# Whole-array transposes and output products, and later stores, in an attention and token-mixing kernel

## The chip, the core and the metric

The kernel runs on one core of a Trainium2 chip. The core has a matrix engine (TensorE; PE for its matmuls, PEld for its weight loads), VectorE (DVE), ScalarE (ACT), GpSimd (POOL) and SyncE (SP), each with its own instruction stream in order, and 16 DMA engines. The metric is device time in microseconds (us).

## The reference

It is a block-wise linear attention with decay, followed by a token-mixing layer. There are 4 batches, 8 heads, 768 positions and 64 columns a head. In the attention, with `Dmask[i, j] = lam ** (i - j)` for `i >= j`:

```python
intra = einsum('bhij,bhjd->bhid', einsum('bhic,bhjc->bhij', qb, kb) * Dmask, vb)
inter = einsum('bhid,bhde->bhie', qb * lam_pow, kv_state)
out[:, :, sl] = intra + inter
kv_state = lam_block * kv_state + einsum('bhsd,bhse->bhde', kb_dec, vb)
```

The heads are then laid side by side, so that `x` is 4 x 768 x 512, and

```python
W_tok = einsum('bsd,btd->bst', x @ w_q, x @ w_k) / 8
out = maximum(einsum('bst,btd->bsd', W_tok, x), 0) @ w_out
```

Inputs and output are float32; the kernel computes in bfloat16 with float32 sums.

## The kernel before

**Pairs.** The work is cut into 16 pairs of heads, n = 0 to 15; batch b = n // 4, pair of the batch kk = n % 4. Positions are cut into six chunks of 128, the decay is folded into q (`Dq`) and v (`DvI`), and one loop over n writes the order of every engine's work out by hand (the pools run under a manual schedule, so program order is engine order).

**What a pair does.** `turn` (L208) transposes q and k of a pair on PE; VectorE writes qT with the decay (L225), ScalarE copies kT (L242). `scores` (L285) makes four PSUM tiles sc, `masks` (L298) multiplies them by the causal mask on VectorE, two tiles each call. `states` (L255) makes the running key-value sums dps; VectorE brings them to gs in three steps (L265 to L267). `inter` (L308) and `values` (L329) add up the attention output in oa, and ScalarE copies it, transposed, to xT (L341). `flip` (L350) transposes xT back to xnat, position-major, copied by ScalarE in batch 0 and for the last pair (L355), else by VectorE (L357).

**Mixing.** Once a batch is whole, `mix_wk` (L371) and `mix_wq` (L390) make the two projections, `mix_py` (L410) the product of wk and x, whose copy is Y (L419, L425). `mix_pm` (L442) makes the mixed rows, ScalarE or VectorE puts them through the relu to rmT (L462, L453). `mix_po` (L473) is the product with w_out, one tile of 128 positions at a time: in `mix_po` and in `flip` each matmul uses 64 columns of weights and writes half of the PSUM partitions, so two are issued for each 128. The tile goes to osb (L484, L482) and is stored by SP at once (L485).

**The order.** The mixing of batch p = b - 1 is spread over the pairs of batch b, by the table at L532: `rows` and `quarters` are calls of `mix_pm`, `one` and `two` are lists of other products that stand in the middle and at the end of a pair's work. For n < 8 a pair's order on PE is rows, scores, wk, states, flip(n-1), one, turn(n+1), inter, quarters, values, two. For n >= 8 it is rows, scores, wk, inter, quarters, flip(n-1), turns, one, values, states(n+1), two (at n = 7 states(8) is made as well). What is left of batches 2 and 3 follows the loop (L587 on).

**Loads.** POOL issues the loads of q, k and v, which turn float32 into bfloat16 on the way (L74, L79), six pairs ahead, and scales v in between (`scale_v`, L193). SP issues the first loads, the weights w_q and w_k, and the stores.

**PSUM.** All tiles but oa come from one pool of six slots (`pst`); a tile waits until the one that held its slot has been read. The output tiles osb have four slots.

Of the kernel before, what the change touches and what calls it, by code (L numbers as in the profile page):

```python
# [27 lines left out]
def kernel(  # L28
# [18 lines left out]
    gsp = ctx.enter_context(tc.tile_pool(name="gsp", bufs=3))  # L47
    xtp = ctx.enter_context(tc.tile_pool(name="xtp", bufs=2))
    hyp = ctx.enter_context(tc.tile_pool(name="hyp", bufs=2))
    outp = ctx.enter_context(tc.tile_pool(name="outp", bufs=4))  # L50
    ps = ctx.enter_context(tc.tile_pool(name="ps", bufs=6, space=bass.MemoryType.PSUM))
    psx = ctx.enter_context(tc.tile_pool(name="psx", bufs=2, space=bass.MemoryType.PSUM))
    ctx.enter_context(tc.manual_schedule())
# [136 lines left out]
    def scale_v(n, eng):  # L190
        b, kk = pairs[n]
        vn = nat.tile([128, 2, NCH, D], BF16, tag="vn", name="vn")
        eng.tensor_tensor(  # L193
            out=vn,
            in0=staged.pop((n, "v")),
            in1=DvI[:, 2 * kk : 2 * kk + 2, :].unsqueeze(3).to_broadcast([128, 2, NCH, D]),
            op=ALU.mult,
        )
        L[n]["vn"] = vn
# [95 lines left out]
    def masks(n, a):  # L295
        for hl in range(2):
            t = prb.tile([128, 3, CH], BF16, tag="pr", name="pr")
            nc.vector.tensor_tensor(out=t, in0=L[n]["sc"][a, hl], in1=maskc, op=ALU.mult)  # L298
            L[n]["pr"][a, hl] = t
# [44 lines left out]
    def flip(n):  # L344
        b, kk = pairs[n]
        xp = pst([128, NCH, CH], BF16, "xp")
        for t in range(NCH):
            for i in range(2):
                o = t * CH + i * 64
                nc.tensor.transpose(  # L350
                    xp[i * 64 : i * 64 + 64, t, :], xT[b][:, kk, o : o + 64], ident
                )
        to = xnat[b][:, :, kk * CH : (kk + 1) * CH]
        if b == 0 or n == N - 1:
            nc.scalar.copy(out=to, in_=xp)  # L355
        else:
            nc.vector.tensor_copy(out=to, in_=xp)  # L357
# [7 lines left out]
    def mix_wk(b, kts=range(NP)):  # L365
        if 0 in kts:
            M[b] = dict(wk=pst([128, NCH, DHY], F32, "wk"))
        wk = M[b]["wk"]
        for t in range(NCH):
            for kt in kts:  # L370
                nc.tensor.matmul(  # L371
                    wk[:, t, :],
                    xT[b][:, kt, t * CH : (t + 1) * CH],
                    wqk[:, 1, kt, :],
                    start=(kt == 0 and (t == 0 or len(kts) == NP)),
                    stop=(kt == NP - 1),
                    skip_group_check=True,
                )
        if NP - 1 in kts:
            wkn = hyp.tile([128, NCH, DHY], BF16, tag="wkn", name="wkn")  # L380
            nc.vector.tensor_copy(out=wkn, in_=wk)
            M[b]["wkn"] = wkn

    def mix_wq(b, kts=range(NP)):
        if 0 in kts:
            M[b]["wq"] = pst([128, HALF], F32, "wq")
        wq = M[b]["wq"]
        for kt in kts:
            for n in range(2):
                nc.tensor.matmul(  # L390
                    wq[n * 64 : n * 64 + 64, :],
                    wqk[:, 0, kt, :],
                    xT[b][:, kt, n * HALF : (n + 1) * HALF],
                    start=(kt == 0),
                    stop=(kt == NP - 1),
                    skip_group_check=True,
                )
        if NP - 1 in kts:
            wqT = hyp.tile([128, HALF], BF16, tag="wqT", name="wqT")
            nc.scalar.copy(  # L400
                out=wqT.rearrange("j (c p r) -> j c r p", c=3, r=2),
                in_=wq.rearrange("j (c r p) -> j c r p", c=3, r=2),
            )
            M[b]["wqT"] = wqT

    def mix_py(b, last=False):
        py = pst([128, 256], F32, "py")
        for t in range(NCH):
            for i in range(2):
                nc.tensor.matmul(  # L410
                    py[i * 64 : i * 64 + 64, :],
                    M[b]["wkn"][:, t, :],
                    xnat[b][:, t, i * 256 : i * 256 + 256],
                    start=(t == 0),
                    stop=(t == NCH - 1),
                    skip_group_check=True,
                )
        Y = hyp.tile([128, 2, 256], BF16, tag="Y", name="Y")
        nc.scalar.copy(out=Y[:, 0, :], in_=py)  # L419
        for i in range(2):  # L420
            o = slice(64 - i * 64, 128 - i * 64)
            if last:
                nc.vector.tensor_copy(out=Y[i * 64 : i * 64 + 64, 1, :], in_=py[o, :])
            else:
                nc.scalar.copy(out=Y[i * 64 : i * 64 + 64, 1, :], in_=py[o, :])  # L425
        M[b]["Y"] = Y
        M[b]["rmT"] = hyp.tile([128, 4, S], BF16, tag="rmT", name="rmT")

    def mix_pm(b, which, wide=True, engs=None):
# [20 lines left out]
        for i, ((dd, n), pm) in enumerate(zip(which, pms)):  # L450
# [10 lines left out]
            else:  # L461
                nc.scalar.activation(out=to, in_=pm, func=ACT.Relu, scale=1.0 / 8.0)  # L462

    def mix_po(b, t, last=False):
        cols = (256, 256) if last and t == NCH - 1 else (HD,)
        osb = outp.tile([128, HD], F32, tag="osb", name="osb")
        c = 0
        for w in cols:
            po = pst([128, w], F32, "po")
            for kt in range(4):  # L470
                for i in range(2):
                    o = t * CH + i * 64
                    nc.tensor.matmul(  # L473
                        po[i * 64 : i * 64 + 64, :],
                        M[b]["rmT"][:, kt, o : o + 64],
                        wo[:, kt, c : c + w],
                        start=(kt == 0),
                        stop=(kt == 3),
                        skip_group_check=True,
                    )  # L480
            if last and (c or (t % 2 and len(cols) == 1)):
                nc.vector.tensor_copy(out=osb[:, c : c + w], in_=po)  # L482
            else:
                nc.scalar.copy(out=osb[:, c : c + w], in_=po)  # L484
            (nc.scalar if len(cols) == 2 and c == 0 else nc.sync).dma_start(  # L485
                out=out[b, t * CH : (t + 1) * CH, c : c + w], in_=osb[:, c : c + w]
            )
            c += w


    warm(WARM2)
# [23 lines left out]
    for n in range(N):  # L515
        b, kk = pairs[n]
        if 8 <= n + 6 < N:
            load_more(n + 6)
        if n + 6 >= N and n + 4 < N:
            scale_v(n + 4, nc.gpsimd)  # L520
        if n == 1:
            load_wqk()
        if n == 3:
            nc.scalar.copy(out=wqk, in_=wqk_f)
        p = b - 1

        def po(b, *ts):
            return [lambda t=t: mix_po(b, t) for t in ts]

        rows, quarters, one, two = {  # L532
            4: ([], [], [lambda: mix_wq(0)], [lambda: mix_py(0)]),
            5: ([], [0, 1], [], []),
            6: ([2], [3], [], po(0, 0, 1)),
            7: ([], [], po(0, 2, 3), po(0, 4, 5)),
        }.get(n, ([], [], [], []))
        if b >= 2:
            rows, quarters, one, two = [
                ([], [], [lambda: mix_wq(p)], [lambda: mix_py(p)]),  # L540
                ([], [0], po(p - 1, 3) if b > 2 else [], po(p - 1, 4) if b > 2 else []),
                ([1], [2], po(p - 1, 5) if b > 2 else [], []),
                ([3], [], [], po(p, 0, 1, 2) if b < B - 1 else po(p, 0, 1)),
            ][kk]
        for dd in rows:
            mix_pm(p, dd)
        scores(n)
        masks(n, 0)
        if b >= 1 and kk == 0:
            mix_wk(p)  # L550
        if n < 8:

            states(n)
            masks(n, 1)
            if n >= 1:
                flip(n - 1)
            for f in one:
                f()
            turn(n + 1)
            if n == 0:  # L560
                scale_v(1, nc.vector)
                make_dq(2)
            if n == 1:
                make_dq(3)
        else:
            masks(n, 1)

        inter(n)
        for dd in quarters:
            mix_pm(p, dd, wide=False)  # L570
        if n >= 8:
            flip(n - 1)
            if 8 <= n <= 9:
                turn(n + 1)
            if n != 8 and n + 2 < N:
                turn(n + 2)
            for f in one:
                f()
        if n == N - 1:
            mix_wk(b, (0, 1, 2))  # L580
            mix_wq(b, (0, 1, 2))
        values(n)
        if n >= 7 and n + 1 < N:
            states(n + 1)
        for f in two:
            f()
    bl = B - 1  # L587
    mix_po(bl - 1, 2)
# [44 lines left out]
```

## Time and profile before

| | |
|---|---|
| median of 10 runs | 105.24 us (104.57 to 106.91) |
| profiled execution, its own time | 105.15 us |
| span of its instructions | 103.1 us |
| packets of the loads' queue | 60400, of the instruction queue 13 |
| landing of v, q, k after issue, median | 6.7, 7.2, 8.2 us |
| landing of a 256 KB store, median | 2.1 us |

A row of the PE timeline has the start, the duration, the engine, the line, what it writes and reads, rows*columns of the array in use, shape and count, and in brackets how long the engine was idle before it and for whom. A matmul's end is modelled, so successive groups overlap in their rows; the step from start to start tells the pace. "issue" is a wait for nothing that the profile shows. The page's part 2 has 40 slices of the span, each digit the busy share in tenths.

### The profile page before, as it was taken

To read this page: it belongs to the slowest core of one execution; us is meant where nothing else is said; L and a number is where in the kernel's file an instruction comes from. 1 tells how busy PE (TensorE), PEld (TensorE's weight loads), DVE (VectorE), ACT (ScalarE), POOL (GpSimd) and SP (SyncE) were. 2 spreads that over 40 slices of the span, in tenths; PEclk is the share of its full clock that TensorE was granted. 3 is DMA by queue.
4 is the path that set the end of the run, shared out by engine and by line. 5 is a ranking of instruction groups with operands and counts; after the bars stand their busy time and mean duration, and the time that the engine had idled before them with its cause. 6 is when DMAs were issued, how large, how long until landed. Compare 5 with 4: busy or idle time off the path is not lost. (4 is left out here: it accounts for less than half of the span.)

```text
span 103.1 us, 3945 instructions
## 1 busy us (share of the span) xinstructions
PE 86.0 (83%) x1714; PEld 59.9 (58%) x1714; DVE 66.1 (64%) x165; ACT 63.7 (62%) x126; POOL 67.5 (65%) x69
## 2 busy tenths in 40 slices
PE   4955887959977889999986895999899889999950
PEld 1324576746856465776964574768585565643530
DVE  3257998894847492965896696649857782264330
ACT  4283658856590969384585884754888825876330
POOL 5999999998999799999979799991320000000000
PEclk9999999999999999999999999999999999999999
DMA  1999999999999999999999999999304120733584
GB/s 24 263 174 157 165 170 160 171 164 162 197 176 164 162 165 168 157 240 260 195 266 169 160 168 163 155 203 266 65 6 154 56 101 0 277 136 134 224 308 149
DMA packets 67410, 17.15 MB, mean 166 GB/s; under 512 B 62914, under 2 KB 64450, under 8 KB 67394
## 3 DMA queue, kind: packets, MB, share of 16 engines
q0 software_dynamic: 60400, 9.57, 125.8%
q1 hardware_dynamic: 6850, 7.21, 21.6%
q8 instruction: 13, 0.21, 0.8%
q10 hardware_dynamic: 144, 0.13, 0.4%
q14 instruction: 3, 0.02, 0.1%
HBM read 20.19 MB, written 6.29 MB: 257 GB/s over the span
## 5 line engine op out<-in xcount | busy, mean ns | idle before, releaser
L298 DVE TENSOR_TENSOR pr<-sc,maskc 128x384 bf16<-128x384 f32 x64 | 32.1, 550 | 11.4 <-PE sc L285 11.4
L193 POOL TENSOR_TENSOR vn<-fv,DvI 128x768 bf16<-128x768 bf16 x14 | 21.0, 1500 | 6.7 <-DMA fv<-in_v_dram 4.3
L473 PE MATMUL po<-wo,rmT 128*64 128x512 bf16 (+1 forms) x200 | 23.0, 371 | 0.1
L242 ACT COPY kT<-trk 128x768 bf16<-128x768 bf16 x16 | 12.8, 800 | 15.1 <-PE trk L238 14.9
L79 POOL DMA_DIRECT2D fv<-in_v_dram x16 | 17.3, 1080 | 0.8 <-POOLq L617 0.8
L484 ACT COPY osb<-po 128x512 f32<-128x512 f32 (+1 forms) x22 | 12.6, 582 | 8.4 <-PE po L473 6.0
L79 POOL DMA_DIRECT2D fk<-in_k_dram x15 | 15.7, 1046 | 0.0
L473 PEld LDWEIGHTS <-rmT 128*64 128x64 bf16 x200 | 10.8, 110 | 8.0 <-ACT rmT L462 0.7
L341 ACT CAST xT<-oa 128x384 bf16<-128x384 f32 x31 | 13.5, 496 | 2.5 <-PE oa L329 2.5
L462 ACT ACTIVATE rmT<-pm 128x384 bf16<-128x384 f32 x28 | 12.3, 506 | 1.6 <-PE pm L442 1.6
L285 PE MATMUL sc<-qT,kT 64*128 64x128 bf16 x192 | 9.8, 217 | 3.8 <-ACT rmT L462 1.0
L74 POOL DMA_DIRECT2D fq<-in_q_dram x15 | 12.8, 852 | 0.0
L285 PEld LDWEIGHTS <-kT 64*128 64x128 bf16 x192 | 6.6, 94 | 7.7 <-issue 4.6
L225 DVE TENSOR_TENSOR qT<-trq,dq 128x768 bf16<-128x768 bf16 x16 | 8.8, 549 | 1.7 <-PE trq L219 1.5
L329 PE MATMUL oa<-pr,vn 128*64 128x128 bf16 x192 | 8.9, 221 | 0.9 <-DVE pr L298 0.5
L238 PE MATMUL trk<-ident,fk 128*64 128x128 bf16 x180 | 7.7, 220 | 2.1 <-DMA fk<-in_k_dram 2.1
L219 PE MATMUL trq<-ident,fq 128*64 128x128 bf16 x192 | 8.5, 220 | 0.6 <-ACT fq L501 0.6
L308 PE MATMUL oa<-qT,gs 64*64 64x128 bf16 x160 | 7.8, 222 | 1.3 <-issue 1.2
L350 PE MATMUL xp<-ident,xT 128*64 128x128 bf16 x192 | 8.4, 221 | 0.4 <-ACT rmT L462 0.4
L329 PEld LDWEIGHTS <-vn 128*64 128x64 bf16 x192 | 6.6, 109 | 3.1 <-issue 1.8
L219 PEld LDWEIGHTS <-fq 128*64 128x64 bf16 x192 | 6.6, 110 | 1.5 <-ACT fq L501 0.7
L442 PE MATMUL pm<-wqT,Y 64*64 64x384 bf16 (+1 forms) x46 | 6.7, 333 | 0.9 <-ACT Y L425 0.6
(59 smaller groups left out, 109.3 us busy)
## 6 DMA issues: line engine op xcount, KB each, us to landing
out_dram<-osb SPq DMA_DIRECT2D x23, 256.0 KB, 2.1
fv<-in_v_dram POOLq DMA_DIRECT2D x16, 192.0 KB, 6.7
fq<-in_q_dram POOLq DMA_DIRECT2D x15, 192.0 KB, 7.2
fk<-in_k_dram POOLq DMA_DIRECT2D x15, 192.0 KB, 8.2
wo<-in_moe_w_out_dram POOLq DMA_DIRECT2D x1, 512.0 KB, 8.5
k<-in_k_dram SPq DMA_DIRECT2D x1, 384.0 KB, 3.4
q<-in_q_dram SPq DMA_DIRECT2D x1, 384.0 KB, 4.8
wqk_f<-in_moe_w_q_dram SPq DMA_DIRECT2D x1, 128.0 KB, 6.4
```

The costliest lines, as they stand in the source:

```text
L74: nc.gpsimd.dma_start(out=t, in_=q_rows(n))
L79: nc.gpsimd.dma_start(out=t, in_=kv_rows(n, dict(k=k, v=v)[nm]))
L193: eng.tensor_tensor(out=vn, in0=staged.pop((n, "v")), in1=DvI[:, 2 * kk : 2 * kk + 2, :].unsqueeze(3).to_broadcast([128, 2, NCH, D]), op=A ...
L219: nc.tensor.transpose(trq[hl * 64 : hl * 64 + 64, a, r, :], fq[:, hl, a, r * D : (r + 1) * D], ident,)
L242: nc.scalar.copy(out=kT, in_=trk)
L285: nc.tensor.matmul(sc[a, hl][:, cc, :], kT[r, c * CH : (c + 1) * CH], qchunk(n, r, c), start=True, stop=True, skip_group_check=True,)
L298: nc.vector.tensor_tensor(out=t, in0=L[n]["sc"][a, hl], in1=maskc, op=ALU.mult)
L329: nc.tensor.matmul(oa[a][r, cc, :], vn[:, hl, c, :], pr[a, hl][:, cc, :], start=False, stop=(cc == 2), skip_group_check=True,)
L341: nc.scalar.copy(out=to, in_=oa[a])
L462: nc.scalar.activation(out=to, in_=pm, func=ACT.Relu, scale=1.0 / 8.0)
L473: nc.tensor.matmul(po[i * 64 : i * 64 + 64, :], M[b]["rmT"][:, kt, o : o + 64], wo[:, kt, c : c + w], start=(kt == 0), stop=(kt == 3), ski ...
L484: nc.scalar.copy(out=osb[:, c : c + w], in_=po)
```

## The change

`flip` and `mix_po` use the whole array: one transpose with 128 columns of weights for two with 64, one matmul of the output product for two. In each pair the flip of the pair before, and the output products that go with it (`whole`), stand right after scores (and wk): for n < 8 ahead of states, for n >= 8 ahead of inter, with the second masks ahead of them. `mix_wq` moves behind states, for n >= 8 behind the turns. The six output products of batch 0 move from pairs 6 (two) and 7 (four) to pairs 7 (four) and 8 (two); those of batch 1 from pairs 11 (three), 13 (two) and 14 (one) to pairs 11 (three), 12 (one) and 13 (two).

Stores are put in a list. Those of batch 0 are held: at n = 8 SP issues a small DMA that reads pair 14's v as it has landed, and the list follows on the same queue; from batch 1 on each `mix_po` empties the list. osb has 14 slots in place of 4.

```diff
-    outp = ctx.enter_context(tc.tile_pool(name="outp", bufs=4))
+    outp = ctx.enter_context(tc.tile_pool(name="outp", bufs=14))
...
-            for i in range(2):
-                o = t * CH + i * 64
-                nc.tensor.transpose(
-                    xp[i * 64 : i * 64 + 64, t, :], xT[b][:, kk, o : o + 64], ident
-                )
+            nc.tensor.transpose(xp[:, t, :], xT[b][:, kk, t * CH : (t + 1) * CH], ident)
...
+    stores = []
+
+    def store():
+        while stores:
+            b, t, c, w, osb = stores.pop(0)
+            (nc.scalar if w < HD and c == 0 else nc.sync).dma_start(
+                out=out[b, t * CH : (t + 1) * CH, c : c + w], in_=osb[:, c : c + w]
+            )
...
-                for i in range(2):
-                    o = t * CH + i * 64
-                    nc.tensor.matmul(
-                        po[i * 64 : i * 64 + 64, :],
-                        M[b]["rmT"][:, kt, o : o + 64],
...
+                nc.tensor.matmul(
+                    po,
+                    M[b]["rmT"][:, kt, t * CH : (t + 1) * CH],
+                    wo[:, kt, c : c + w],
+                    start=(kt == 0),
+                    stop=(kt == 3),
+                )
...
+            stores.append((b, t, c, w, osb))
             c += w
+        if b > 0:
+            store()
...
+        if n == 8:
+
+            late = consts.tile([1, D], BF16, name="late")
+            nc.sync.dma_start(out=late, in_=staged[n + 6, "v"][0:1, 0, 0, :])
+            store()
...
+        rows, quarters, whole, cols = {
+            4: ([], [], [], [lambda: mix_py(0)]),
             5: ([], [0, 1], [], []),
-            6: ([2], [3], [], po(0, 0, 1)),
-            7: ([], [], po(0, 2, 3), po(0, 4, 5)),
+            6: ([2], [3], [], []),
+            7: ([], [], po(0, 0, 1, 2, 3), []),
+            8: ([], [], po(0, 4, 5), [lambda: mix_py(p)]),
         }.get(n, ([], [], [], []))
-        if b >= 2:
...
+        if n > 8:
+            rows, quarters, whole, cols = [
+                ([], [], po(p - 1, 3), [lambda: mix_py(p)]),
+                ([], [0], po(p - 1, 4, 5) if b > 2 else [], []),
+                ([1], [2], [], []),
+                ([3], [], po(p, 0, 1, 2) if b < B - 1 else po(p, 0, 1), []),
             ][kk]
...
         if b >= 1 and kk == 0:
             mix_wk(p)
+        if n >= 8:
+            masks(n, 1)
+        if n >= 1:
+            flip(n - 1)
+        for f in whole:
+            f()
         if n < 8:
 
             states(n)
             masks(n, 1)
-            if n >= 1:
-                flip(n - 1)
-            for f in one:
-                f()
+            if kk == 0 and b:
+                mix_wq(p)
             turn(n + 1)
...
         if n >= 8:
-            flip(n - 1)
...
+            if kk == 0:
+                mix_wq(p)
...
-        for f in two:
+        for f in cols:
             f()
```

More of the change, by code (lines that the diff above doesn't have):

```diff
@@ L470, in mix_po @@
             for kt in range(4):
-                for i in range(2):
-                    o = t * CH + i * 64
-                    nc.tensor.matmul(
-                        po[i * 64 : i * 64 + 64, :],
-                        M[b]["rmT"][:, kt, o : o + 64],
[L476 to L480, printed above, removed]
+                nc.tensor.matmul(
[5 more added lines that the diff above has]
+                )
             if last and (c or (t % 2 and len(cols) == 1)):
@@ L484, in mix_po @@
                 nc.scalar.copy(out=osb[:, c : c + w], in_=po)
-            (nc.scalar if len(cols) == 2 and c == 0 else nc.sync).dma_start(
-                out=out[b, t * CH : (t + 1) * CH, c : c + w], in_=osb[:, c : c + w]
-            )
+            stores.append((b, t, c, w, osb))
             c += w
+        if b > 0:
+            store()
     warm(WARM2)
@@ L528, in po @@
             return [lambda t=t: mix_po(b, t) for t in ts]
-        rows, quarters, one, two = {
-            4: ([], [], [lambda: mix_wq(0)], [lambda: mix_py(0)]),
+        rows, quarters, whole, cols = {
+            4: ([], [], [], [lambda: mix_py(0)]),
             5: ([], [0, 1], [], []),
-            6: ([2], [3], [], po(0, 0, 1)),
-            7: ([], [], po(0, 2, 3), po(0, 4, 5)),
+            6: ([2], [3], [], []),
+            7: ([], [], po(0, 0, 1, 2, 3), []),
+            8: ([], [], po(0, 4, 5), [lambda: mix_py(p)]),
         }.get(n, ([], [], [], []))
-        if b >= 2:
[L539 to L543, printed above, removed]
+        if n > 8:
[4 more added lines that the diff above has]
+                ([3], [], po(p, 0, 1, 2) if b < B - 1 else po(p, 0, 1), []),
             ][kk]
@@ L564 @@
                 make_dq(3)
-        else:
-            masks(n, 1)
         inter(n)
@@ L576 @@
                 turn(n + 2)
-            for f in one:
-                f()
+            if kk == 0:
+                mix_wq(p)
         if n == N - 1:
```

## The prediction

> **What bounds the kernel now.** I read the page first, then the PE timeline pair by pair, the waits, and the timeline of all engines around pairs 5 to 8.
>
> ```profile
> PE 86.0 (83%) x1714; PEld 59.9 (58%) x1714; DVE 66.1 (64%) x165; ACT 63.7 (62%) x126; POOL 67.5 (65%) x69
> ...
> PEclk9999999999999999999999999999999999999999
> DMA  1999999999999999999999999999304120733584
> ...
> q8 instruction: 13, 0.21, 0.8%
> ```
>
> No share reaches 100%, but PE is the spine: from pair 8 on its rows abut, except at a few named gaps. The DMA engines are full until about 72 us. The q8 line is instruction fetch: 13 packets for some 3,430 TensorE instructions, about 256 each.
>
> The PE timeline, cut to pairs 9 to 11 (start, duration, then what; idle time in brackets):
>
> ```profile
> 51.97 0.51 PE L285 MATMUL sc<-qT,kT 64*128 64x128 bf16 x12
> ...
> 52.71 0.32 PE L442 MATMUL pm<-wqT,Y 64*64 64x384 bf16 x1
> 53.30 0.35 PE L442 MATMUL pm<-wqT,Y 64*64 64x384 bf16 x3 [0.27 <-ACT Y L425]
> ...
> 54.28 0.50 PE L238 MATMUL trk<-ident,fk 128*64 128x128 bf16 x12
> 54.82 0.53 PE L219 MATMUL trq<-ident,fq 128*64 128x128 bf16 x12
> 55.91 0.53 PE L238 MATMUL trk<-ident,fk 128*64 128x128 bf16 x12 [0.56 <-DMA fk<-in_k_dram]
> 56.89 0.53 PE L329 MATMUL oa<-pr,vn 128*64 128x128 bf16 x12 [0.46 <-issue]
> ...
> 63.64 0.30 PE L308 MATMUL oa<-qT,gs 64*64 64x128 bf16 x4 [1.16 <-issue]
> ```
>
> Brackets use modelled ends; I use starts. Twelve half-width matmuls take 0.34, so pair 9 loses 0.59 to Y, 0.20 and 0.75 to pair 11's q and k, 0.64 to "issue"; pair 11 loses 1.33 to "issue". The matmuls from 56.89 to the 63.64 row number exactly 128, that is 256 instructions with their weight loads: both stalls are at block ends, as is the 0.81 at 31.04 (512 matmuls before 56.89). The next block is late because its packet is: cut to 54.5 to 55.6 and to 61.1 to 62.1 us, the DMA view shows one instruction packet each, 1.4 to 1.5 us before PE goes on.
>
> **Prices.** *Mode change.* Six pairs of py go to po (both 128*64) in 0.65 (89.78 to 90.43) but to scores (64*128) in 0.76 (51.21 to 51.97): 0.11. A wq pair goes to whole-array wk in 0.26, not 0.16: 0.10. So whole-array is a mode of its own, at 0.11 a change.
> *Flip.* Twelve half-width transposes take 0.35 (48.95 to 49.30), because two halves run side by side. Six whole ones are not in the trace: as low as wk's whole-array matmuls of 64 columns (24 in 0.70: 0.17 a flip), as high as two halves in sequence (0.70). wk's 98 ns weight loads hide behind a 29 ns spacing, so loads add nothing; nearest is a half pair of 128 columns. I take 0.35, a gain of nothing; the ends are -2.9 and +5.6 for 16 flips.
> *Output product.* Three take 2.69 less a mode change: 0.86 each, 0.216 a step of 512 columns; the two whole-array warm-ups at 6.47 and 6.69 stand 0.22 apart. Gain nothing, within 0.1 in all.
>
> The Trainium skill speaks against the flips ("TensorE: Matmul & The Clock Gate", Part 4: PE-mode transpose): a full 128x128 transpose took some 275 ns inside a kernel. By that, an estimate, a flip would take 1.65 and the time would pass 125. The half-width rows here, 58 ns a pair in the same transpose operation, don't support it, and no run here shows a whole one.
>
> So the array does the same work at the same rate. What changes is order, instruction count (12 fewer a flip, 8 fewer an output product: 392) and mode changes. Pairs 1, 2, 3, 5, 6, 7, 9, 10, 11, 13, 14 get one change more (whole between scores and the next mode); 4, 8, 12, which have wk there, and 15 none; the tail three more.
>
> The wq product moves by a few groups within pairs 4, 8 and 12; its copy (0.60 on ScalarE) is first needed by pm one pair later: nothing.
>
> **Pairs 0 to 5: nothing.** Flip ahead of states makes states wait for xT: pair 2 loses some 0.45 on VectorE's chain. But pair 4's k lands at 22.89 and pair 6's at 32.80, and PE waits for both (1.07 and 0.48); no store is out yet, so these landings stay and swallow it. The fetch stall at 31.04 also ends before 32.80.
>
> **Pairs 6 to 8: a loss.** All engines, pairs 6 and 7:
>
> ```profile
> 35.61 0.91 ACT L341 CAST xT<-oa 128x384 bf16<-128x384 f32 x2
> 36.65 0.23 DVE L265 COPY two<-dps 128x64 f32<-128x64 f32 x1
> 37.25 1.01 DVE L298 TENSOR_TENSOR pr<-sc,maskc 128x384 bf16<-128x384 f32 x2
> 38.18 0.55 DVE L357 COPY xnat<-xp 128x768 bf16<-128x768 bf16 x1
> 38.65 0.55 DVE L225 TENSOR_TENSOR qT<-trq,dq 128x768 bf16<-128x768 bf16 x1
> 39.01 1.89 PE L473 MATMUL po<-wo,rmT 128*64 128x512 bf16 x16
> 40.83 0.51 PE L285 MATMUL sc<-qT,kT 64*128 64x128 bf16 x12
> ```
>
> Now VectorE's 4 us a pair hide beside two output products. After: flip 5 starts when xT is copied (36.52), ends on VectorE's side at 37.1; then, in its new order, xnat 0.55, two and gs 0.69, masks 1.01, qT 0.55: scores of pair 7 at 39.85, with no output product done. Pair 7: xT of 6 is ready at 40.7 (kT 0.80, rmT 0.88, xT 0.87 in a row), flip to 41.1, four products at 0.863 to 44.55, change and states to 44.9. Two, gs and second masks now stand behind those products on VectorE: 45.1 + 0.69 + 1.0 + 0.55 puts scores of pair 8 at 47.4; before, 47.30 with all six done. Pair 8 carries the other two: 4.67 as before + 1.73. Pair 9's scores move from 51.97 to 53.8: **+1.83**. The cover that is gone is the products in pair 6.
>
> **Pair 9 on.** Y: flip (and from batch 2 two products) stands before the first pm, so 0.45 of 0.59 goes in pair 9 and all 0.64 in pair 13 (73.59 to 74.23): **-1.09**. Loads: PE wants pair 11's q and k over 1 us later than before, so both waits go even if they land no sooner: **-0.95**. Fetch: see below, **-1.97**. Mode changes: five pairs and three in the tail, 8 x 0.11 = **+0.88**. Pair 12 has no products before wk now: kT 0.80 and xT 0.43 start 0.2 after the last transpose, PE is at wk 1.2 after it: **+0.3**. Flips directly after scores wait for xT (0.2 + 0.80 + 0.87 = 1.9 after the last transpose, scores end at 1.4 or later) and for a PSUM slot at pairs 10, 11, 14, 15; scores wait there already (0.29, 0.22, 0.23, 0.80: 1.54). Between all that going (-1.5) and 0.4 each on top (+1.6), nearest to what stands there is a swap of one wait for the other: **+0.3**.
>
> **Fetch and stores.** By count of matmuls the three late blocks came 6.2, 7.0 and 6.75 us after PE entered the block before, which fits a request at that point; PE's work in a block lasts 5.4 in pairs 9 to 11. Landing times are the measure: 9 us for q and k issued at 20 to 25 us, 5.6 to 6.1 by 35 to 40, 8 to 9.8 again with stores (41 to 55). Without stores POOL issues a pair every 4.33 us, the DMA moves one in some 3.6 (0.59 MB at 164 GB/s), so by 50 us the backlog is gone and a block comes in 4 to 5. Of 392 instructions fewer, 144 fall ahead of pair 9, and pairs 7 and 8 last longer. So both stalls go (other end: one of 1.1 stays, 6.2 for a block that then has 5.1 of work, in pair 10; elsewhere blocks last 6.7 or more).
> The new wait is SP's: `late` waits for pair 14's v (issued 63.09, lands by about 70). Behind it on SP stand four stores of batch 0 and then all of batch 1; only osb slots wait for those, and 14 slots come round at batch 2's third tile, near 87 us. The burst falls on 66 to 75 us, where pair 15's v is the last load and has until 80: nothing. Were SP held beyond 87, ScalarE's copies would wait.
>
> **Sum.** +1.83 - 1.09 - 0.95 - 1.97 + 0.88 + 0.3 + 0.3 = -0.7 on the profiled execution's 105.15 (span 103.1 and 2.05 around it); the median is 0.09 above it. Forecast 104.5.
>
> **Rivals.** *One fetch stall stays* (the loads alone keep the DMA full; for: it is full at 25 to 40 us without stores; against: landings fall to 5.6): +1.1, 105.6, no change. *The flips wait*: if xT's second copy, behind kT on ScalarE, ends 0.5 after scores on pairs 10, 11, 12, 14 and the old slot waits stay too, it costs 4 x 0.5 on top: 106.5, slower. It decides where kT starts later than the last transpose + 0.2; for it: ACT's kT row waits 14.9 us for trk, so xT queues behind it; against: from 57.6 on scores themselves end late. *The change does not shift the work as I read it*, pairs 6 to 8 lose nothing since VectorE finds xnat and masks in time: 102.7.
>
> **Chances.** Forecast 0.47 (103.7 to 104.7), fetch stall 0.22, flips wait 0.25, no loss 0.06. Faster by over 0.5% (what a measurement here can tell): 0.53, within 0.22, slower 0.25. The range 103.2 to 106.4 leaves out the last case and the upper part of the slower one; the flip's far ends are excluded by the hidden weight loads and the side-by-side rows.
>
> **What would show it.** Six transposes in 0.35 and products at 0.86; no "issue" gap after 50 us; no wait for q or k after 33; pair 8's scores at 47.4 and pair 9's near 53.8; gaps before xp named ACT xT or rmT. Wrong if whole transposes are slower than 58 ns, if "issue" gaps remain, or if pair 12's scores are later than 68.2.

## The result and the profile after

The changed kernel takes 106.13 us (median of 14 runs, 105.94 to 107.67) against 105.44 for the kernel before on the same chip: a ratio of 1.0095 with a 95% interval of 1.0061 to 1.0129. A second set of 10 runs gave 106.1 and 1.0064 (1.0023 to 1.0105). So it is slower by 0.6 to 1%, where 104.5 and faster was forecast. Three of the 14 runs, the profiled one among them, were slow ones (107.58 to 107.67) and don't count in the ratio. All that follows is read from the profile of the second set, whose span is 104.1 (before: 103.1). From pair 6's scores to the end of the span the two profiles of the changed kernel agree to 0.01 (68.43 and 68.44). The first lost its 1.6 in pairs 3 to 5, where it waited for a loaded v (0.86) and k (0.78).

The page of the changed kernel, the same lines as for before:

```profile
PE 90.2 (87%) x1518; PEld 59.1 (57%) x1518; DVE 66.4 (64%) x165; ACT 64.3 (62%) x126; POOL 67.5 (65%) x69
...
PEclk9999999999999999999999999999999999999999
DMA  0999999999999999999999999999943005132584
...
q8 instruction: 11, 0.18, 0.7%
```

PE has 196 matmuls (392 instructions with their loads) and two instruction packets fewer, at a granted clock of 1.00, and yet its busy time has risen. The DMA engines stay full for one slice (2.6 us) more.

The PE timeline of the changed kernel from pair 9's scores on, cut to what the prediction spoke of:

```profile
53.82 0.51 PE L285 MATMUL sc<-qT,kT 64*128 64x128 bf16 x12
54.26 0.51 PE L348 MATMUL xp<-ident,xT 128*128 128x128 bf16 x6
...
57.72 0.50 PE L285 MATMUL sc<-qT,kT 64*128 64x128 bf16 x7
58.40 0.34 PE L285 MATMUL sc<-qT,kT 64*128 64x128 bf16 x5 [0.18 <-DVE gs L267]
59.16 0.49 PE L348 MATMUL xp<-ident,xT 128*128 128x128 bf16 x6 [0.43 <-ACT rmT L458]
...
62.39 0.34 PE L285 MATMUL sc<-qT,kT 64*128 64x128 bf16 x5 [0.21 <-DVE gs L267]
63.12 0.50 PE L348 MATMUL xp<-ident,xT 128*128 128x128 bf16 x6 [0.39 <-ACT rmT L458]
...
75.18 1.89 PE L476 MATMUL po<-wo,rmT 128*128 128x512 bf16 x8 [0.42 <-ACT Y L421]
...
80.52 0.50 PE L348 MATMUL xp<-ident,xT 128*128 128x128 bf16 x6 [0.39 <-ACT rmT L458]
```

No "issue" row and no wait for q or k is left after pair 6. In their place stand waits in brackets that before had not in these pairs: flips wait for rmT, a product waits for Y, and the old wait of the scores for gs is still there.

Cut into steps from a pair's first scores to the next pair's, the two profiles give, in us:

| from | before | after | difference | forecast, with the swap's +0.3 left out |
|---|---|---|---|---|
| pairs 6 to 8 | 16.79 | 18.17 | +1.38 | +1.83 |
| pair 9 | 5.81 | 3.90 | -1.91 | -1.93 (Y, loads, fetch, a mode change) |
| pair 10 | 3.40 | 3.99 | +0.59 | +0.11 |
| pair 11 | 7.00 | 6.25 | -0.75 | -1.22 (fetch, a mode change) |
| pair 12 | 4.67 | 5.85 | +1.18 | +1.16 (a product moved here, 0.86, and 0.3) |
| pair 13 | 5.29 | 5.31 | +0.02 | -0.53 (Y, a mode change) |
| pair 14 | 3.52 | 3.28 | -0.24 | -0.75 (the product moved away, a mode change) |
| pair 15 to the end | 21.46 | 21.70 | +0.24 | +0.33 |
| sum from pair 6 | 67.93 | 68.44 | +0.51 | -1.00, with the swap -0.70 |

The rest of the longer span is the start: pair 6's scores stand at 35.65, before at 35.18. That moves from run to run (see the end), so experiments are compared by the stretch from pair 6's scores to the end of the span as well as by their medians. Each stretch is that of one profiled run.

In short, two readings competed. **A: ScalarE's queue is late next.** With the stalls gone, PE runs into PSUM slots that rmT's copies on ScalarE still hold, and into xT behind them; the new order puts the flip just there. **B: the whole-array form itself is slow**, or its mode changes are. For pairs 6 to 8 the rivals were the lost cover of the products and VectorE's new order.

### The profile page after: what moved, and what is told of

Read it like the earlier page. It is cut to its first block, busy times and chain, and to the rows that moved or that the text cites. A ratio compares the mean times of both kernels' runs of the same rounds, so it can differ in the third digit from the quotient of the medians.

```text
span 105.7 us, 3540 instructions
## 1 busy us (share of the span) xinstructions
PE 90.3 (85%) x1510; PEld 59.7 (56%) x1518; DVE 66.3 (63%) x165; ACT 64.3 (61%) x126; POOL 67.5 (64%) x69
## 3 DMA queue, kind: packets, MB, share of 16 engines
HBM read 20.19 MB, written 6.29 MB: 250 GB/s over the span
## 4 chain that ended last, share of the span: by engine, by line
PE 39%; ACT 21%; DMA 18%; POOL 14%; issue 2%; DVE 2%; POOLq 0%; ACTq 0%
PE po L476 19%; DMA fv<-in_v_dram 9%; DMA fk<-in_k_dram 8%; ACT rmT L458 8%; ACT kT L242 6%; ACT xT L341 5%; POOL fv L79 4%; PE xp L348 4%; POOL fq L74 3%; POOL fk L79 3%; PE oa L308 3%; PE wk L367 2%; PE trk L238 2%; PE trq L219 2%; PE wq L386 1%
## 5 line engine op out<-in xcount | busy, mean ns | idle before, releaser
L476 PE MATMUL po<-wo,rmT 128*128 128x512 bf16 (+1 forms) x92 | 22.3, 370 | 1.0 <-ACT Y L421 0.4
L476 PEld LDWEIGHTS <-rmT 128*128 128x128 bf16 x100 | 9.2, 98 | 10.4 <-issue 1.3
L348 PE MATMUL xp<-ident,xT 128*128 128x128 bf16 x96 | 8.7, 220 | 2.5 <-ACT rmT L458 1.2
L329 PE MATMUL oa<-pr,vn 128*64 128x128 bf16 x192 | 9.4, 227 | 0.8 <-DVE pr L298 0.7
L219 PE MATMUL trq<-ident,fq 128*64 128x128 bf16 x192 | 9.3, 233 | 0.6 <-ACT xnat L351 0.5
L265 DVE COPY two<-dps 128x64 f32<-128x64 f32 x16 | 3.6, 224 | 9.7 <-PE dps L255 9.4
L348 PEld LDWEIGHTS <-xT 128*128 128x128 bf16 x96 | 5.8, 97 | 4.8 <-ACT xT L341 2.6
```

The costliest lines, as they stand in the source:

```text
L219: nc.tensor.transpose(trq[hl * 64 : hl * 64 + 64, a, r, :], fq[:, hl, a, r * D : (r + 1) * D], ident,)
L329: nc.tensor.matmul(oa[a][r, cc, :], vn[:, hl, c, :], pr[a, hl][:, cc, :], start=False, stop=(cc == 2), skip_group_check=True,)
L348: nc.tensor.transpose(xp[:, t, :], xT[b][:, kk, t * CH : (t + 1) * CH], ident)
L476: nc.tensor.matmul(po, M[b]["rmT"][:, kt, t * CH : (t + 1) * CH], wo[:, kt, c : c + w], start=(kt == 0), stop=(kt == 3),)
```

## The experiments

**The same kernel again** (no edit).

> The changed kernel once more, for its time beside the others on the same chip and for a profile with TensorE's clock up from the start. All theories: 105.9 to 106.3; scores of pair 6 within 0.6 of before's 35.18 if the early loss of the profile at hand is the cold clock, 1 us or more later if it is the order.

Median 106.1, stretch 68.44. The loss is real, and its size is that of the first runs. The question of the start was not settled by it: PE starts as slowly in this profile as in the first (twelve half-width transposes take 0.62 from 11.11 on in both, but 0.33 from 10.23 on in before), while the granted clock stands at 1.00 in all three.

**Held stores alone, in the kernel before** (14 osb slots, the list of stores, `late` at n = 8).

> The kernel before with the held stores and the 14 output slots alone; order and half-width matmuls as before. Theory A (the stores choke the loads and the instruction fetch): the waits for pair 11's q and k (0.95) go, and the two fetch stalls of 1.33 and 0.64 shrink or go: 1.0 to 2.9 us faster, 102.5 to 104.5. Theory B (the fetch stalls went in the changed kernel because it has fewer instructions and longer blocks, not because of the stores): only the 0.95 goes and part of it is lost to the fetch, the stalls near pair 9 to 11 stay over 0.5 each: 0 to 1 us faster.

```diff
+            stores.append((b, t, c, w, osb))
+        if b > 0:
+            store()
...
+        if n == 8:
+            late = consts.tile([1, D], BF16, name="late")
+            nc.sync.dma_start(out=late, in_=staged[n + 6, "v"][0:1, 0, 0, :])
+            store()
```

Median 103.5, ratio 0.9795 (0.9759 to 0.9831), stretch 65.49. Its page and PE timeline, pairs 10 and 11:

```profile
q8 instruction: 13, 0.21, 0.9%
```

```profile
57.04 0.50 PE L285 MATMUL sc<-qT,kT 64*128 64x128 bf16 x7
57.72 0.34 PE L285 MATMUL sc<-qT,kT 64*128 64x128 bf16 x5 [0.18 <-DVE gs L267]
57.99 0.47 PE L308 MATMUL oa<-qT,gs 64*64 64x128 bf16 x10
58.48 0.74 PE L442 MATMUL pm<-wqT,Y 64*64 64x384 bf16 x4
59.15 0.53 PE L350 MATMUL xp<-ident,xT 128*64 128x128 bf16 x12
...
61.04 0.46 PE L285 MATMUL sc<-qT,kT 64*128 64x128 bf16 x7
```

Thirteen packets and 392 instructions more than the changed kernel, as before the change, and no "issue" row after 33 us, no wait for pair 11's q and k: the stores' traffic, not the count of instructions alone, made the fetches and loads late. But pair 10 takes 4.00 (57.04 to 61.04) where it took 3.40. The four quarters of pm, 0.36 without a wait (55.21 in the changed kernel), stretch to 0.74, which reads as a wait for PSUM slots: two kT copies (from 55.77, 1.50) now stand ahead of rmT's on ScalarE where before one did (56.47, 0.80), and rmT starts 1.03 after its pm (57.90 for 56.87), before 0.43 (58.04 for 57.61). So 0.6 of the 2.8 gained in pairs 9 and 11 is given back, with no flip moved. It is given back in pair 10 alone: pair 11 takes 5.77, where 5.67 is left without its stall, and pair 14 takes 3.47 for 3.52.

**Whole-array matmuls alone, in the old order; and with held stores.**

> The kernel before with whole-array flips and output products alone, in the old order, where they stand between half-width groups. Mode changes at 0.11: some 20 more from pair 6 on, 2.2 us; 392 instructions fewer give back up to 1 us of fetch stalls. If a mode change is the only price of the form: 0.7 to 2.5 us slower, with flips at 0.35 and products at 0.86. If whole-array transposes were slower as such: flips over 0.45 each in the PE rows.

> The held stores with whole-array flips and products, in the old order (hold_only plus whole_only). Theory A (the whole form costs its mode changes, 0.11 each and some 20 from pair 6 on; whole_only came out level because its 392 instructions fewer also took the fetch stalls away, which the held stores have already done here): slower than hold_only by 1.2 to 2.2 us, 104.7 to 105.7. Theory D (mode changes cost next to nothing in sum): within 0.6 us of hold_only, 102.9 to 104.1.

```diff
-            for i in range(2):
-                o = t * CH + i * 64
-                nc.tensor.transpose(
-                    xp[i * 64 : i * 64 + 64, t, :], xT[b][:, kk, o : o + 64], ident
-                )
+            nc.tensor.transpose(xp[:, t, :], xT[b][:, kk, t * CH : (t + 1) * CH], ident)
```

(and the output products likewise). Without held stores 106.54, ratio 1.0025 (0.9969 to 1.0081), stretch 68.82; with them 105.81, 1.0046 (0.9964 to 1.0127), stretch 67.07, which is 1.58 more than held stores alone. The PE timeline of the first, pair 9:

```profile
55.79 0.53 PE L219 MATMUL trq<-ident,fq 128*64 128x128 bf16 x12 [0.19 <-DMA fq<-in_q_dram]
...
57.03 0.53 PE L238 MATMUL trk<-ident,fk 128*64 128x128 bf16 x12 [0.72 <-DMA fk<-in_k_dram]
```

With fewer instructions alone the "issue" rows go too, while the loads stay late; that gain hides the loss by the form: by the medians the kernel is level with before, and in the stretch 0.9 of loss is left. So this run alone would have misled. The pair with held stores shows the loss plainly. Counted from pair 6's scores on, PE changes between rows*columns 41 times in half width and 60 times with the whole array in the old order: 1.58 over 19 is 0.083 a change. It falls where the changes are: pairs 8, 9, 10 and 12 have one more each and take 0.10 to 0.11 longer, pair 13 has four more and takes 0.44 longer. In the new order PE changes 51 times.

**The new order with half-width matmuls.**

> The changed kernel with its new order and held stores, but flips and output products as half-width pairs again. Theory A (the order is what costs: VectorE's chain in pairs 6 to 8 and the flips' wait for a PSUM slot): the time stays within 0.7 us of the changed kernel's, 105.4 to 106.3, since only mode changes in pairs 1 to 7 and in the tail (some 0.55 that count) go. Theory C (the whole-array form is what costs): it falls by more than 1 us, to 105 or below.

Median 107.58, ratio 1.0132 (1.0069 to 1.0194), stretch 68.98. So with the new order, half width is no better: the mode changes saved are few (48 for 51), and the same waits stand in its timeline (0.39 for rmT before three flips, 0.41 for Y). With the instructions back a fetch is late once (0.53, "issue", at 38.56), and pairs 6 and 7 take 0.64 more than in the changed kernel; the tail takes 0.47 less. The median is over what either theory expected, and the profiled run was the fastest of its six. Reading B can't carry the loss of the changed kernel. Against held stores alone, with the same half-width form, this run also shows what the place of the flip does: pair 11 takes 6.29 for 5.77, of which a mode change is 0.1, and its flip waits 0.39 for rmT, where the other has no wait.

**The change without holding stores.**

> The changed kernel, but stores at once as before. Theory A (the held stores are worth what they save in load waits and fetch stalls, and in the new order pairs 7 and 8 last longer and have fewer instructions, so little of it is left): 0 to 1 us slower than the changed kernel, 106.0 to 107.1, with a wait for pair 11's k or q or one stall of issue after 50 us. If the hold is worth the same in either order: 2 us slower, 108.

```diff
-        if b > 0:
-            store()
+        store()
```

(and `late` gone). 106.92, ratio 1.0115 (1.003 to 1.02, from 4 runs), stretch 68.59 against 68.44. What is worth 2.4 in the old order (67.93 to 65.49) is worth 0.14 in the new: the two remedies act on the same stalls and don't add.

**Products of batch 0 back to the ends of pairs 6 and 7.**

> The changed kernel with the six products of batch 0 at the end of pairs 6 (two) and 7 (four), behind values, instead of ahead of states in pairs 7 and 8. Theory A (VectorE's chain in pairs 6 to 8 lost its cover): from the first scores of pair 6 to those of pair 9 it takes 17.0 instead of 18.2, and the whole is 1.0 to 1.5 us faster than the changed kernel, 104.6 to 105.1. Rival E (flip ahead of states alone makes that loss): 0.4 us faster or less.

```diff
-            6: ([2], [3], [], []),
-            7: ([], [], po(0, 0, 1, 2, 3), []),
-            8: ([], [], po(0, 4, 5), [lambda: mix_py(p)]),
+            6: ([2], [3], [], po(0, 0, 1)),
+            7: ([], [], [], po(0, 2, 3, 4, 5)),
+            8: ([], [], [], [lambda: mix_py(p)]),
```

106.47, ratio 1.0082 (1.0047 to 1.0116), stretch 68.47: nothing of the 1.0 to 1.5 expected. Pairs 6 to 8 take 18.20 for 18.17. Its pair 6 is 6.03; less two products of 0.864 that is 4.30, against 4.40 with none. The cover that the prediction named, products in pair 6, hid some 0.1 of that pair. Its PE timeline in pair 7:

```profile
42.03 0.51 PE L285 MATMUL sc<-qT,kT 64*128 64x128 bf16 x12
42.47 0.51 PE L348 MATMUL xp<-ident,xT 128*128 128x128 bf16 x6
42.91 0.45 PE L255 MATMUL dps<-vn,fk 128*64 128x128 bf16 x10
...
44.27 0.62 PE L308 MATMUL oa<-qT,gs 64*64 64x128 bf16 x10 [0.24 <-DVE gs L266]
```

Scores and flip now go in 0.44 each, where the changed kernel takes 0.60 (40.05 to 40.65) and 0.56 (40.65 to 41.21). But no product stands between the states and inter any more, and inter waits for gs: one wait for another, 0.28 against some 0.3 (trk to inter 0.74 for 0.43).

**States and second masks ahead of the flip and the products, for n < 8.**

> The changed kernel, but for n < 8 states and the second masks stand ahead of flip and of the products again; all else as changed. Rival E, now the theory (flip ahead of states lengthens the chain scores, xT, flip, states, gs, masks, qT, and PE has nothing to do beside it): first scores of pair 6 to those of pair 9 in 16.8 to 17.3 instead of 18.2, the whole 1.0 to 1.4 us faster than the changed kernel, 104.6 to 105.1. Theory A (missing products in pair 6 and four in a row in pair 7): 18 in these pairs, no faster than 0.4 us.

```diff
+        if n < 8:
+            states(n)
+            masks(n, 1)
         if n >= 1:
             flip(n - 1)
         for f in whole:
             f()
         if n < 8:
-            states(n)
-            masks(n, 1)
```

105.71, ratio 0.9985 (0.9951 to 1.0019), stretch 67.82, pairs 6 to 8 17.57: 0.60 of the 1.38 was this order, about half of what was expected of it. First rows of VectorE and of the weight loads in the changed kernel, then all engines in this one, both pair 7:

```profile
41.41 0.56 DVE L353 COPY xnat<-xp 128x768 bf16<-128x768 bf16 x1
45.24 0.22 DVE L265 COPY two<-dps 128x64 f32<-128x64 f32 x1 [3.28 <-PE dps L255]
```

```profile
40.64 0.17 PEld L348 LDWEIGHTS <-xT 128*128 128x128 bf16 x3 [0.26 <-ACT xT L341]
...
41.02 0.17 PEld L348 LDWEIGHTS <-xT 128*128 128x128 bf16 x3 [0.21 <-ACT xT L341]
```

```profile
39.56 0.88 ACT L458 ACTIVATE rmT<-pm 128x384 bf16<-128x384 f32 x2
...
39.77 0.66 PE L285 MATMUL sc<-qT,kT 64*128 64x128 bf16 x12
...
40.31 0.88 ACT L341 CAST xT<-oa 128x384 bf16<-128x384 f32 x2
...
40.36 0.45 PE L255 MATMUL dps<-vn,fk 128*64 128x128 bf16 x10
40.86 0.17 PEld L348 LDWEIGHTS <-xT 128*128 128x128 bf16 x3 [0.19 <-ACT xT L341]
40.87 0.72 PE L348 MATMUL xp<-ident,xT 128*128 128x128 bf16 x6
...
41.24 0.17 PEld L348 LDWEIGHTS <-xT 128*128 128x128 bf16 x3 [0.21 <-ACT xT L341]
```

VectorE stood idle for 3.28 while the four products ran ahead of the states, as the prediction said. With the states first that idle time is gone, and pair 7 is still 7.10 against 6.47: scores take 0.59 to the next row, where 0.44 is usual (40.83 to 41.27 in before), and the flip 0.56, where 0.33 is (48.58 to 48.91 after wk). ScalarE's rmT and xT run from 39.56 to 41.19, and the flip's weight loads wait for xT by name, 0.19 and 0.21 (0.26 and 0.21 in the changed kernel). Before, rmT and xT ran beside the output products at the end of pair 6. These two rows are 0.38 long in excess, and pairs 6 and 7 have four mode changes more than before, some 0.4: together the 0.78 that is left. That sum is of rows, and no run takes the two apart.

**The rows of pm behind scores and first masks, for n >= 8, in the changed kernel.** A row's rmT copies then free their slots after the scores have theirs.

> The changed kernel with the rows part of mix_pm behind scores and the first masks for n >= 8, so that its two PSUM slots are taken after those of scores. Theory A (the flips of pairs 10, 11 and 14 wait 0.4 each, and the scores of pair 15 wait 0.8, for slots that rmT's copies free late): these gaps named ACT rmT go, 1.0 to 2.0 us faster, 104.1 to 105.1. Rival F (the flips would wait for xT just as long): within 0.5 us, the gaps are then named ACT xT or DVE.

```diff
+        if n < 8:
             for dd in rows:
                 mix_pm(p, dd)
         scores(n)
         masks(n, 0)
+        if n >= 8:
+            for dd in rows:
+                mix_pm(p, dd)
```

105.6, ratio 0.9993 (0.9942 to 1.0045), stretch 67.33: 1.11 less, and pairs 10 and 11 go from 3.99 and 6.25 to 3.68 and 6.11. (Pair 11's step now holds its own row of 0.17, which stood in pair 10's step; so it, too, gains 0.3.) ScalarE and PE at pair 10 of the changed kernel, then PE in this one:

```profile
56.45 1.50 ACT L242 COPY kT<-trk 128x768 bf16<-128x768 bf16 x2
...
57.55 0.34 PE L438 MATMUL pm<-wqT,Y 64*128 64x384 bf16 x2
...
57.84 0.88 ACT L341 CAST xT<-oa 128x384 bf16<-128x384 f32 x2
...
58.58 0.92 ACT L458 ACTIVATE rmT<-pm 128x384 bf16<-128x384 f32 x2
...
59.16 0.49 PE L348 MATMUL xp<-ident,xT 128*128 128x128 bf16 x6 [0.43 <-ACT rmT L458]
```

```profile
57.81 0.51 PE L285 MATMUL sc<-qT,kT 64*128 64x128 bf16 x12
58.27 0.73 PE L438 MATMUL pm<-wqT,Y 64*128 64x384 bf16 x2
59.12 0.49 PE L348 MATMUL xp<-ident,xT 128*128 128x128 bf16 x6
```

In the changed kernel pm is made at 57.55, but kT and xT stand ahead of its copies on ScalarE, so its slots are held past 59. xT is whole at 58.72, when the scores are through: the flip at 59.16 waits for a slot, not for xT. With the row behind the scores, the scores run in one group, their wait for gs (0.18) is gone, and no wait stands before the flip; the row itself is longer (0.73 for 0.34), as its second weight load now waits 0.46 for gs. Of the 1.11, some 0.7 is won in pairs 10, 11 and 14 (in 14 only 0.06) and 0.4 in pair 15, where the old wait of 0.80 was.

**The same move with held stores in the old order, and with fillers for Y.**

> hold_only, half-width in the old order, with the rows part of mix_pm behind scores for n >= 8, so that no slot hangs on rmT's copies: the gaps of pair 10 (0.6 at the quarters' pm), of scores in pairs 10, 11, 14 (0.2 each) and of pair 15 (0.8) should go: 0.8 to 1.8 us faster than hold_only, 101.7 to 102.7. If xT or VectorE is as late as rmT: 103 or above.

> hold_rows_late with flip (and in pair 13 the product) of pairs 9 and 13 between scores and inter, where PE waits for Y's copies: 0.6 in each pair less one or two mode changes of 0.11: 0.3 to 0.9 us faster than hold_rows_late. If the wait only moves to the flip or the product: no faster.

```diff
+        early = n in (9, 13)
+        if early:
+            flip(n - 1)
+            for f in one:
+                f()
```

(ahead of inter, and not again behind it.) The first gives 102.67, ratio 0.9692 (0.9631 to 0.9753), stretch 64.64, 0.85 under held stores alone; pair 10 is 3.72 for 4.00. The second 102.11, 0.9657 (0.9604 to 0.9711), stretch 64.40. Both beat both kernels. The fillers' own gain is within the intervals, and the spans are equal at 100.1. By pairs it is plain which one fills: pair 9, with the flip, takes 3.76 for 4.06; pair 13, where a product follows the flip, takes 5.17 for 5.12, and the product waits 0.41 for Y.

**Both repairs of order in the changed kernel.**

> The changed kernel with both repairs of order together: the rows of mix_pm behind the scores and first masks for n >= 8, and the states with the second masks ahead of the flip and the products for n < 8. Alone the first took 1.11 us off the stretch from pair 6's scores to the end of the span (67.33 for 68.44) and the second 0.62 (67.82). Theory, that they act in different pairs (9 on, and 6 and 7) and add up: 66.7 in that stretch, and a median near 104.8 us, 0.993 of the kernel before, between it and the held stores alone in the old order. What then remains against the kernel with held stores and late rows alone (64.63) is 2.1 us: the mode changes of the whole arrays (1.6 by the run of held stores with whole arrays), and the products of batch 0 that stand in pairs 7 and 8. Rival, that time saved in pairs 6 and 7 is given back at pairs 9 to 11 as the changed kernel gave back its fetch stalls: 67.3, and no gain over the late rows alone (105.6).

104.71, ratio 0.9919 (0.9888 to 0.9951), stretch 66.72: the two add up (68.44 - 1.11 - 0.62 = 66.71). The changed kernel, its order mended at two places, comes near the time that was forecast for it. That is partly chance: the late rows also take away a wait of 0.8 in pair 15 that the forecast had left in place.

## Why the prediction was wrong

By the order of the sum, with loads and fetch together and the rates last:

1. **Pairs 6 to 8, +1.83: right in sign, +1.38 measured; the cover was misnamed.** VectorE waited for dps as described, but the order of flip and products before states was worth 0.60 of it. Putting products back into pair 6 brought nothing. The other 0.78 reads as mode changes and as pair 7's waits for ScalarE's rmT and xT, which the products at the end of pair 6 had stood beside; a product at that place frees the waits of the changed kernel there (0.28) and uncovers gs.
2. **Y, -1.09: half right.** Pair 9's part came: its whole step was forecast at -1.93 and measured at -1.91. Pair 13's 0.64 did not: the filler that should have hidden Y, a product, waits for Y itself (75.18, 0.42), since it needs a PSUM slot that py holds until Y is copied. Only the flip is free of that. The step went from 5.29 to 5.31 where 4.76 was due.
3. **Loads -0.95 and fetch -1.97: right.** All four stalls went, and two experiments each removed the "issue" rows by another way. That the gain of holding the stores would not survive in the new order is what the sum could not show, as it gave each term once.
4. **Mode changes, +0.88: right.** The eight more from pair 9 on are there; at 0.083 to 0.11 each they make 0.66 to 0.88.
5. **Pair 12, +0.3: right** (+1.18 with the product of 0.86 that moved there).
6. **The swap at pairs 10, 11, 14 and 15, +0.3: this step failed.** It reads "a swap of one wait for the other", between -1.5 and +1.6. Measured, with the terms above taken off: +0.48, +0.47, +0.51 and, with the tail, -0.09, in all +1.37. In pairs 10, 11 and 14 the new waits came on top and the old ones stayed; in each, the flip waits some 0.4 for a slot that an rmT copy frees. Two causes bring this about. In pair 10 the waits of pair 9 had given ScalarE time to catch up; with them gone, its kT, xT and rmT copies come last, and held stores alone show the same loss with no flip moved (4.00 for 3.40). In pairs 11 and 14 they do not show it (5.77 where 5.67 was left, 3.47 for 3.52): there the flip's new place, straight behind the scores, makes PE ask for the slot before rmT is copied. With half-width matmuls and held stores in both, pair 11 takes 6.29 in the new order and 5.77 in the old. Moving the rows takes some 0.7 of the 1.46 in these three pairs back. Why it brings so little in pair 14 (0.06) stays open.
7. **Rates: right.** Six whole transposes take 0.33 (48.58 to 48.91), 55 ns each, and 16 product steps 3.55 with a mode change. The 275 ns that the Trainium skill gives for one transpose in a kernel ("TensorE: Matmul & The Clock Gate", Part 4: PE-mode transpose) is the time of one instruction. Here one takes 219 ns by the trace's modelled ends, but six overlap: a flip is 0.33, not the 1.65 of that estimate.

Terms 2 and 6 are 0.55 and 1.07 worse than forecast, term 1 is 0.45 better, the rest within 0.05: from -0.70 to +0.51. The rival "the flips wait" named three of the right pairs (10, 11 and 14; in its fourth, 12, no wait stands) and had very nearly the time (106.5), but in those pairs not the mechanism. It priced xT's copy; what these flips wait for is a slot that rmT's copy frees (59.16, with xT whole at 58.72). For xT itself the flip of pair 7 waits. Its condition, kT late behind the transposes, was in the prediction, with the row for it, and the argument against it (the scores end late themselves) was the wrong one: they do end late, by their wait for gs (0.18 at 58.40), and the flip waits 0.43 more.

Pairs 0 to 5 are not settled. The changed kernel loses about 1.6 in pairs 1 and 2 against before (4.37 and 4.48 for 3.79 and 3.42), and wins most of it back by pair 6, where it stands between before (35.18) and held stores alone, with the same order as before (36.02). But over six profiles in the old order pair 6's scores come at 35.0 to 36.0, mean 35.5, and over six with the flip ahead of the states at 35.3 to 37.3, mean 36.1: a loss of some 0.5 is not excluded. The burst of held stores shows in no wait of the engines: `late` goes out at 66.1 and lands 2.5 later.

## What to carry to other kernels

When a change removes stalls of one kind, ask which in-order engine used them to catch up; price its queue before the gain is booked. When work moves forward, ask which slot it takes and who must free it. A filler that takes a buffer from the same pool as the thing waited for is no filler. Price a gain that two parts of a change both bring only once, and run each part alone: here holding the stores alone was worth 2%, and with the rest of the change nothing of it was left.

## What the runs showed of the hardware

A change of the rows*columns in use cost PE 0.08 to 0.11 us here, whether the whole array or half of it followed, and 19 of them made 1.6. A late instruction block was cured by less DMA traffic (13 packets, no "issue" row after 33 us) as by fewer instructions (11 packets, with the stores still in the way). And the start of PE's work moves from run to run: the first scores came between 9.08 and 9.79 us in these profiles, with no clear effect on pair 6, ahead of which PE mostly waits for a k: 9.08 led to 35.18, 9.09 to 36.00, 9.74 to 35.65.
